# The second norm's sums of three chunks go from VectorE to ScalarE, and the transposes behind them come three groups sooner

## The chip, the cores and the metric

The kernel runs on one core of a Trainium2 chip, as one program. The metric is the time of one execution in microseconds (us), as a median of runs on the chip. A profile of one execution shows every instruction of the engines: TensorE (PE for its products, PEld for its weight loads), VectorE (DVE), ScalarE (ACT), GpSimd (POOL) and the queue of SyncE (SP).

## The reference

A transformer block with adaptive norms, on 2048 rows of 512 numbers, in float32:

```python
mod = (_silu(c) @ w_mod).reshape(c.shape[0], 6, 1, -1)
sa, ca, ga, sb, cb, gb = (mod[:, 0], mod[:, 1], mod[:, 2], mod[:, 3], mod[:, 4], mod[:, 5])
h = _layernorm(x, axis=-1) * (1 + ca) + sa
x = x + ga * _A_ref(h, A_wqkv, A_wo)              # softmax attention, 32 heads of 16
h = _layernorm(x, axis=-1) * (1 + cb) + sb        # the second norm
x = x + gb * _B_ref(h, B_w_gate, B_w_up, B_w_down)  # (silu(h wg) * (h wu)) wd, inner width 1792
return x
```

`_layernorm` subtracts the mean of a row of 512 and divides by the root of its variance plus 1e-5.

## The kernel before, in words

The rows are cut into 4 chunks of 512, each of 4 tiles of 128 rows. After the first norm and the projections (`proj_T`, `proj_v`), the attention runs as one long sequence of steps: 32 units (4 chunks times 8 groups of 4 heads) of 16 steps, and 4 pairs a step. A pair (`pair_of`) issues one score product with its exponential (`score`: TensorE L569, ScalarE L571) and, some 20 steps ahead of it, one product for the row maximum with its reduction (`max_one`: TensorE L521, VectorE L523). The products of the exponentials with v (`pv_step`, L584) follow in bundles of half steps (`pvs`). At the end of a unit `close_unit` copies the result (L588) and queues loads on SP and POOL.

While a chunk's attention runs, the rest of the block for the chunk before it is done between the pairs. That gives two kinds of stretch:

- `plain(steps)`: only attention, in groups of three pairs and then products with v. Four PSUM banks take the products for the maxima in a ring (0 to 3, begun anew by each call of `plain`), three take the scores. A function in `tails` is called in a group between its pairs and its products with v, with the next bank of the ring of four.
- `filled(places, work)`: eight pairs, with products of `work` between them as `places` says, then four half steps of v. Three banks take the maxima here, two the scores, and banks 3 and 6 the outputs of `work`.

For each of the first three chunks the loop at the end of the kernel goes: `plain` up to a fixed step; `out_pair` for tiles 0 and 1 in two filled stretches, then for tiles 2 and 3 in two more (the output projection, L782); `plain(NORM)`, 9 steps or 12 groups; `plain(WIN)`, 3 steps or 4 groups; for the third chunk a further `plain(REST)`; and then the gate, up and down products in filled stretches. The document counts the 16 groups behind the four stretches from 0.

The second norm lies around these. When an `out_pair` is done, `add_o` adds it to x (VectorE L804, two tiles), and `sums` takes mean and variance of a tile (VectorE L808 and L809). `scaled` then loads the first gate weights, forms one over the root in small operations (`norm_scale`: VectorE L740 to L742, then POOL L749 to L754), and normalizes the four tiles on POOL (`normalize`, L761). `turned` transposes a block of 128 columns of the four tiles on TensorE (L766), scales and shifts it on ScalarE (L768), and splits it in a high and a low part on POOL (L769, L770).

Three lists set when such work is issued. `side` gives up one entry behind each pair. `posts` is emptied at the end of each filled stretch (`hook`). `behind` holds entries with a count; at the end of each group and each filled stretch (`turns_behind`, after the products with v) each count falls by one, and an entry whose count reaches zero is issued. Instructions are issued in this written order, and each engine works through its own in that order. The fourth chunk's norm runs alone at the end, with `late` false and VectorE for `norm_scale`.

Of the kernel before, what the change touches and what calls it, by code (L numbers as in the profile page):

```python
# [13 lines left out]
AF = mybir.ActivationFunctionType  # L14
ALU = mybir.AluOpType
# [6 lines left out]
D = 512  # L22
# [4 lines left out]
NK = D // P  # L27
# [6 lines left out]
EPS = 1e-5  # L34
# [5 lines left out]
WIN = 3  # L40
# [7 lines left out]
NORM = 9  # L48
# [53 lines left out]
def block_kernel(ctx, tc, x, wqkv, wo, w_gate, w_up, w_down, c, w_mod, out):  # L102
    nc = tc.nc
# [18 lines left out]
    four, bank, single = Turn(0, 1, 2, 3), Turn(4, 5, 6), Turn(7)  # L122
# [271 lines left out]
    def proj_T(ci, w, m, by=1, aside=False):  # L394
        def job():
            pt = bank("pt")
            col = (0 if w == 0 else D) + m * P

            def post():
                prt = pa0.tile([P, 2, CW], F32R, name="prt", tag="prt", bufs=4)  # L400
                if aside:
                    full = prt[:, 1, :].bitcast(F32)
                    nc.scalar.copy(full, pt)
                    yield
                    nc.gpsimd.tensor_copy(prt[:, 0, :], full)
                    nc.gpsimd.tensor_sub(prt[:, 1, :], full, prt[:, 0, :].bitcast(F32))
                else:
                    nc.scalar.copy(prt[:, 0, :], pt)
                    yield
                    nc.vector.tensor_sub(prt[:, 1, :], pt, prt[:, 0, :].bitcast(F32))  # L410
                yield
                dst = (qd, kd)[w][m * P:(m + 1) * P, :, ci * CW:(ci + 1) * CW]
                nc.sync.dma_start(dst[:, 1 - w:3 - w, :], prt.bitcast(F32))
                nc.sync.dma_start(dst[:, 2 * w, :], prt[:, 0, :].bitcast(F32))
            return mm3(pt, lambda a, k: wqs[a][:, k, col:col + P], lambda b, k: hT[ci][b][:, k, :], NK, by, w == 1), post()
        return job
# [77 lines left out]
    posts, behind = [], []  # L494
# [134 lines left out]
    def tile_mid():  # L629
        return pf.tile([P, 2, CW], F32R, name="mid", tag="mid", bufs=3)  # L630

    def tmp(name):
        return pf.tile([P, CW], F32, name=name, tag="tmp", bufs=4)
# [56 lines left out]
    class Chunk:  # L690
# [45 lines left out]
        def norm_scale(self, eng):  # L736

            mv, rs, a = self.mv, self.rs, self.rs2[:, 0]
            va = mv[:, :, 1]
            nc.vector.tensor_scalar_add(va, va, EPS)  # L740
            nc.vector.tensor_scalar(rs.bitcast(I32), va.bitcast(I32), 1, None, op0=ALU.logical_shift_right)
            nc.vector.tensor_scalar(rs.bitcast(I32), rs.bitcast(I32), -1, 0x5f3759df, op0=ALU.mult, op1=ALU.add)  # L742
            for _ in range(3):
                if eng is nc.vector:
                    eng.scalar_tensor_tensor(a, rs, -0.5, rs, op0=ALU.mult, op1=ALU.mult)
                    eng.tensor_mul(a, a, va)
                    eng.scalar_tensor_tensor(rs, a, 1.5, rs, op0=ALU.add, op1=ALU.mult)
                else:
                    eng.tensor_mul(a, rs, rs)  # L749
                    eng.tensor_mul(a, a, va)  # L750
                    eng.tensor_scalar(a, a, -0.5, 1.5, op0=ALU.mult, op1=ALU.add)
                    eng.tensor_mul(rs, rs, a)
            eng.tensor_mul(self.rs2[:, 1], mv[:, :, 0], rs)
            eng.tensor_scalar_mul(self.rs2[:, 1], self.rs2[:, 1], -1.0)  # L754

        def normalize(self, t, alone=False):
            if alone:
# [39 lines left out]
    def add_o(ch, t0, outs, late):  # L797
        if ch.mv is None:
            ch.mv = pf.tile([P, 4, 2], F32, name="mv2", tag="mv2", bufs=1)
            ch.rs = pf.tile([P, 4], F32, name="rs", tag="rs", bufs=1)  # L800
            ch.rs2 = pf.tile([P, 2, 4], F32, name="rs2", tag="rs2", bufs=1)
        for e in range(2):
            t = t0 + e
            nc.vector.tensor_add(ch.x2[:, t, :], outs[e], ch.x2[:, t, :])  # L804

        def sums(t):
            st = pf.tile([P, 6], F32, name="stt", tag="stt", bufs=2)
            nc.vector.bn_stats(st, ch.x2[:, t, :])  # L808
            nc.vector.bn_aggr(ch.mv[:, t, :], st)  # L809

        for e in range(2):
            if late:
                side.append(lambda t=t0 + e: sums(t))
            else:
                sums(t0 + e)

    def out_pair(ch, t0, outs, halves):
        return accumulate(outs, lambda e, a, k: ch.oT[a][:, k, (t0 + e) * P:(t0 + e + 1) * P],
                          lambda b, k: ch.wo[k // 2][:, b, k % 2, :], NK,
                          lambda: posts.append(lambda: add_o(ch, t0, outs, True)), halves)  # L820
# [53 lines left out]
    side = []  # L874
# [13 lines left out]
    def scaled(ch):  # L888
        ch.load_gu(0)
        ch.norm_scale(nc.gpsimd)  # L890
        ch.nt = [tile_mid().bitcast(F32) for _ in range(2)]
        for t in range(4):
            ch.normalize(t)
# [7 lines left out]
    late = sm.jobs([proj_T(last, *kq[0])] + [(late_t if w == "T" else late_v).pop(0) for w in "TTVTVTTVTTVTTVVVV"])  # L901
# [3 lines left out]
    four, bank = Turn(0, 1, 2, 3, 6, 7), Turn(4, 5)  # L905
# [56 lines left out]
    def pair_of():  # L962
        nonlocal done
        i = done // 4 - 1
        most = 4 * n - 4 * (LEAD - 1)
        h = (ORDER if done < most else (0, 1, 2, 3))[done % 4]
        work = [lambda: score(i + 1, h)]
        if done < most:
            work.insert(1 - h % 2, lambda: max_one(done + 4 * (LEAD - 1)))
        for f in work:  # L970
            f()
        done += 1
        if side:
            side.pop(0)()

    for i in range(-LEAD, -1):
# [7 lines left out]
        if i == -2:  # L984
            four, work = three, bank
# [11 lines left out]
    def pvs(most, by_halves):  # L997

        nonlocal owed
        if by_halves:  # L1000
            most, owed = most + owed, 0
        while most and halves and 4 * halves[0][0] + 8 <= done:
            i, half = halves.pop(0)
            pv_step(i, half)
            most -= 1
            if i % 16 == 15 and half:
                close_unit(i // 16, done // 4 - 1)
                if by_halves:
                    break
        if by_halves and most and halves and 4 * halves[0][0] + 8 <= done:  # L1010
            owed = most

    def turns_behind():
        for b in list(behind):
            b[0] -= 1
            if not b[0]:
                b[1]()
                behind.remove(b)

    def end_steps():  # L1020
        nonlocal ended
        while ended < done // 4:
            after(ended - 1)
            ended += 1

    def plain(steps, tails=()):

        nonlocal four, bank, beside
        beside = False
        assert steps % WIN == 0 and done % 4 == 0  # L1030
        four, bank = Turn(0, 1, 2, 3), Turn(4, 5, 6)
        for w in range(4 * steps // WIN):
            for _ in range(WIN):
                pair_of()
            if w >= 4 * steps // WIN - len(tails):
                tails[w - 4 * steps // WIN](four())
            pvs((HALVES[(w - 2) % 4] if done > 8 else 0) + (w == 4 * steps // WIN - 1), True)
            turns_behind()
            end_steps()
# [30 lines left out]
    for ci in range(last):  # L1070
        plain(STARTS[ci] - done // 4)
        ch = chunks[ci]
        for t0 in (0, 2):
            work = out_pair(ch, t0, outs, True)
            filled(TWO, work)
            filled(TWO, work)
        side.append(lambda: scaled(ch))
        plain(NORM)
        plain(WIN, [lambda tp, k=k: ch.turned(tp, k) for k in range(NK)])
        if ci == last - 1:  # L1080
            plain(REST)
        for _ in range(len(ch.jobs) - (KEEP if ci == last - 1 else 0)):
            job, args = ch.jobs.pop(0)
            if args == (NF // FG - 1, 0):
                plain(WIN)
            work = job(ch, *args, outs, True)
            for places in (TWO, TWO) if job is gate_up else (DOWN,):
                filled(places, work)
# [5 lines left out]
    turns = chain([2, 3, 2, 0, 1, 2, 0], cycle([1, 3, 2, 0]))  # L1094
# [19 lines left out]
    ch, chp = chunks[last], chunks[last - 1]  # L1114
# [10 lines left out]
    for t in range(4):  # L1125
        out_terms(ch, t, banks[t], (NK - 1,))
        if t % 2:
            add_o(ch, t - 1, banks[t - 1:t + 1], False)
# [40 lines left out]
```

## Time and profile before

| | |
|---|---|
| median of 3 runs | 1834.48 us (1833.5 to 1835.62) |
| the profiled execution's own time | 1835.76 us |
| its span in the profile | 1833.9 us |
| mean granted TensorE clock | 0.998 |
| busy: PE, DVE, ACT, POOL | 1821.6, 1530.4, 1241.4, 460.8 us |

A row of a timeline gives the start and the length in us, engine, line, operation, output and input, a count where rows are merged, and in brackets the idle time before it with what ended it. A row of a group of instructions gives the busy time in us, the mean ns of one, and the idle time of the engine before them. The chain is the work that ended last, followed back from the end of the program.

### The profile page before, as it was taken

The numbers are of one execution on the slowest core, as the hardware profiler recorded it, in microseconds if no ns is written. First come the engines' busy times: TensorE is split into PE (matmuls) and PEld (weight loads), VectorE is DVE, ScalarE is ACT, GpSimd is POOL, SyncE is SP. The second block draws the span as 40 slices with busy tenths as digits, with TensorE's granted clock in tenths as the row PEclk, the third lists the DMA queues.
The fourth block names the chain that finished last, engine by engine and source line by source line (L and its number), as shares of the span: only waits on it lengthen the run. The fifth ranks groups of instructions, "written<-read, shape, count | busy, mean of one in ns | idle before, by whom it ended". The sixth has DMA issues, their size and how long they took to land.

```text
span 1833.9 us, 41048 instructions
## 1 busy us (share of the span) xinstructions
PE 1821.6 (99%) x16904; PEld 1199.0 (65%) x16904; DVE 1530.4 (83%) x2578; ACT 1241.4 (68%) x2386; POOL 460.8 (25%) x541
## 2 busy tenths in 40 slices
PE   9999999999999999999999999999999999999999
PEld 7876444444455777776565777776564577767887
DVE  5578999999999888889999888889999988831544
ACT  4223888888877777777878777777878877774211
POOL 3612544565223111111123111111123011130200
PEclk9999999999999999999999999999999999999999
DMA  9784776657845444453544554454643545333642
GB/s 311 281 225 154 180 184 199 168 188 171 220 79 126 102 118 143 118 143 73 146 104 108 133 129 120 119 121 84 163 83 57 112 92 150 139 120 122 272 169 110
DMA packets 80488, 267.63 MB, mean 146 GB/s; under 512 B 19604, under 2 KB 24212, under 8 KB 59620
## 3 DMA queue, kind: packets, MB, share of 16 engines
q1 hardware_dynamic: 61324, 179.71, 34.0%
q0 software_dynamic: 18288, 84.49, 19.3%
q8 instruction: 133, 2.18, 0.5%
q10 hardware_dynamic: 688, 0.80, 0.1%
q14 instruction: 55, 0.45, 0.1%
HBM read 201.85 MB, written 62.13 MB: 144 GB/s over the span
## 4 chain that ended last, share of the span: by engine, by line
PE 82%; DVE 16%; DMA 1%; ACT 0%; issue 0%; SPq 0%; DVEq 0%
PE bank L584 21%; PE bank L782 19%; DVE mx L523 15%; PE bank L569 14%; PE bank L521 11%; PE bank L792 8%; PE bank L211 7%; PE bank L825 1%; PE bank L766 0%; DMA wm_ab<-in_w_mod 0%; DVE stt L808 0%; DMA qop<-mr 0%; PE bank L163 0%; DVE v_flat L856 0%; PE bank L535 0%
## 5 line engine op out<-in xcount | busy, mean ns | idle before, releaser
L523 DVE TENSOR_REDUCE mx<-bank 128x1 f32<-128x512 f32 x2048 | 1274.3, 685 | 108.7 <-PE bank L521 68.0
L569 PE MATMUL bank<-qop,kop 50*128 50x512 f32 x2048 | 728.8, 426 | 2.5 <-DMA qop<-mr 1.6
L521 PE MATMUL bank<-kop,qop 48*128 48x512 f32 x2048 | 727.0, 426 | 2.5 <-DVE mx L523 2.1
L569 PEld LDWEIGHTS bank<-qop,kop 50*128 50x128 f32 x2048 | 343.5, 184 | 169.8 <-issue 53.6
L521 PEld LDWEIGHTS bank<-kop,qop 48*128 48x128 f32 x2048 | 343.9, 185 | 113.3 <-DVE mx L523 68.7
L782 PE MATMUL bank<-act,wgu 64*128 64x512 f32 x1872 | 301.5, 392 | 0.0
L782 PEld LDWEIGHTS bank<-act,wgu 64*128 64x128 f32 x1872 | 196.7, 187 | 24.2 <-issue 0.2
L611 POOL TENSOR_TENSOR on<-o,rb 128x512 f32<-128x512 f32 x31 | 39.8, 1285 | 494.9 <-DMA rb<-d_dr 350.3
L782 PE MATMUL bank<-wd,mid 64*128 64x512 f32 x912 | 133.8, 397 | 0.0
L844 POOL CAST mid<-m 128x512 fp32r<-128x512 f32 x40 | 24.3, 608 | 381.7 <-DVE m L842 239.2
L782 PEld LDWEIGHTS bank<-wd,mid 64*128 64x128 f32 x912 | 87.7, 185 | 16.1 <-ACT first L879 3.1
L211 PE MATMUL bank<-hT,wqs 128*128 128x512 f32 x384 | 94.3, 397 | 0.4 <-DVE wqs L351 0.4
L840 DVE SCALAR_TENSOR_TENSOR q<-th,bank 128x512 f32<-128x512 f32 x56 | 38.3, 683 | 54.1 <-ACT th L836 54.1
L211 PEld LDWEIGHTS bank<-hT,wqs 128*128 128x128 f32 x384 | 70.6, 188 | 18.8 <-issue 3.0
L836 ACT ACTIVATE th<-bank 128x512 f32<-128x512 f32 x56 | 33.2, 594 | 57.9 <-PE bank L792 57.9
L856 DVE TENSOR_TENSOR x<-bank,x 128x512 f32<-128x512 f32 x84 | 53.9, 685 | 18.3 <-PE bank L782 16.7
L842 DVE TENSOR_TENSOR m<-bank,q 128x512 f32<-128x512 f32 x56 | 38.7, 692 | 21.7 <-PE bank L792 19.7
L845 POOL TENSOR_TENSOR mid<-m,mid 128x512 fp32r<-128x512 f32 x40 | 51.5, 1287 | 3.3
L792 PE MATMUL bank<-wd,mid 128*128 128x512 f32 x216 | 51.3, 393 | 0.0
L782 PE MATMUL bank<-wgu,act 64*128 64x512 f32 x288 | 48.0, 394 | 0.1
L211 PE MATMUL bank<-wqs,hT 128*128 128x512 f32 x192 | 48.0, 398 | 0.0
L792 PEld LDWEIGHTS bank<-wd,mid 128*128 128x128 f32 x216 | 40.4, 188 | 8.9
(6298 smaller groups left out, 5139.7 us busy)
## 6 DMA issues: line engine op xcount, KB each, us to landing
wgu<-gu_dr SPq DMA_DIRECT2D x48, 1024.0 KB
wd<-wd_dr SPq DMA_DIRECT2D x28, 1024.0 KB
kop<-kd SPq DMA_DIRECT2D x33, 768.0 KB
kop<-kd POOLq DMA_DIRECT2D x29, 768.0 KB, 8.9
gu_dr<-wgu POOLq DMA_DIRECT2D x14, 1024.0 KB, 13.8
kd<-prt SPq DMA_DIRECT2D x16, 512.0 KB
qd<-prt SPq DMA_DIRECT2D x16, 512.0 KB
kop<-gu_dr SPq DMA_DIRECT2D x8, 1024.0 KB
```

The lines of the kernel that those rows point to most:

```text
L211: nc.tensor.matmul(pt, lhs(a, k), rhs(b, k), start=(n == 0), stop=(n == 3 * nk - 1))
L521: nc.tensor.matmul(pm, qop[u][rows, s, qt * P:(qt + 1) * P], kop[u % 3][rows, s, kc * CW:(kc + 1) * CW], start=True, stop=True)
L523: nc.vector.tensor_reduce(mx[u][:, b, s, qt, kc:kc + 1], pm, op=ALU.max, axis=AX.X)
L569: nc.tensor.matmul(sp, kop[u % 3][rows, h // 2, kt * P:(kt + 1) * P], qop[u][rows, h // 2, :], start=True, stop=True)
L584: nc.tensor.matmul(pv[u][32 * h:32 * h + 32, cols], v_flat[:, e0:e0 + 32], p_[h][:, cols], start=(kt == 0 and half == 0), stop=(kt == 15), ...
L611: mul.tensor_mul(on, o, rb)
L782: nc.tensor.matmul(outs[e], lhs(e, a, k)[rows], rhs(b, k)[rows], start=(ph == 0 and j == 0), stop=(j == z and (ph == 1 or trade is not None)),
L792: nc.tensor.matmul(outs[e], lhs(e, a, k), rhs(b, k), start=(j == 0), stop=(j == z))
L840: nc.vector.scalar_tensor_tensor(q, th, 1.0, outs[0], op0=ALU.add, op1=ALU.mult)
L842: nc.vector.tensor_mul(m32, outs[1], q)
L845: (nc.gpsimd if slow else nc.vector).tensor_sub(mid[:, 1, :], m32, mid[:, 0, :].bitcast(F32))
L856: nc.vector.tensor_add(ch.x2[:, t, :], outs[e], ch.x2[:, t, :])
```

## The change

For the first three chunks the sums of a tile are no longer one VectorE statistic of two instructions but two ScalarE passes over the tile, each of which adds up its outputs into one column: `minus_mean` scales by −1/512 and sums, which gives minus the mean; `squares` takes that as its bias, squares and sums. The passes are put on `behind`, for tiles 0 and 1 with the counts 1, 2, 2, 3 and for tiles 2 and 3 with 1, 2, 3, 4. `scaled` goes from `side` to `behind` with the count 4, that is, behind the fourth group. `norm_scale` divides the sum of squares by 512 in the instruction that adds the 1e-5, and for these chunks leaves out the POOL multiplication by −1. The four calls of `turned` move from the four groups of `plain(WIN)` to the last three of `plain(NORM)` and the first of `plain(WIN)`. The fourth chunk is as before.

```diff
             va = mv[:, :, 1]
-            nc.vector.tensor_scalar_add(va, va, EPS)
+            if eng is nc.vector:
+                nc.vector.tensor_scalar_add(va, va, EPS)
+            else:
+                nc.vector.tensor_scalar(va, va, 1.0 / D, EPS, op0=ALU.mult, op1=ALU.add)
...
             eng.tensor_mul(self.rs2[:, 1], mv[:, :, 0], rs)
-            eng.tensor_scalar_mul(self.rs2[:, 1], self.rs2[:, 1], -1.0)
+            if eng is nc.vector:
+                eng.tensor_scalar_mul(self.rs2[:, 1], self.rs2[:, 1], -1.0)
...
-        for e in range(2):
-            if late:
-                side.append(lambda t=t0 + e: sums(t))
-            else:
+        def minus_mean(t):
+            nc.scalar.activation(tmp("sq"), ch.x2[:, t, :], AF.Identity, scale=-1.0 / D,
+                                 accum_out=ch.mv[:, t, 0:1])
+
+        def squares(t):
+            nc.scalar.activation(tmp("sq"), ch.x2[:, t, :], AF.Square, bias=ch.mv[:, t, 0:1],
+                                 accum_out=ch.mv[:, t, 1:2])
+
+        if late:
+            turns = (1, 2, 2, 3) if t0 == 0 else (1, 2, 3, 4)
+            works = ((minus_mean, t0), (squares, t0), (minus_mean, t0 + 1), (squares, t0 + 1))
+            behind.extend([k, lambda f=f, t=t: f(t)] for k, (f, t) in zip(turns, works))
+        else:
+            for e in range(2):
                 sums(t0 + e)
...
-            if w >= 4 * steps // WIN - len(tails):
-                tails[w - 4 * steps // WIN](four())
+            if w < len(tails) and tails[w]:
+                tails[w](four())
...
-        side.append(lambda: scaled(ch))
-        plain(NORM)
-        plain(WIN, [lambda tp, k=k: ch.turned(tp, k) for k in range(NK)])
+        behind.append([4, lambda: scaled(ch)])
+        tails = [lambda tp, k=k: ch.turned(tp, k) for k in range(NK)]
+        plain(NORM, [None] * NORM + tails[:3])
+        plain(WIN, tails[3:])
```

## The prediction

> **What bounds the kernel now.** I read the page first, for the engines' shares and the chain that ended last.
>
> ```profile
> span 1833.9 us, 41048 instructions
> ...
> PE 1821.6 (99%) x16904; PEld 1199.0 (65%) x16904; DVE 1530.4 (83%) x2578; ACT 1241.4 (68%) x2386; POOL 460.8 (25%) x541
> ...
> PE 82%; DVE 16%; DMA 1%; ACT 0%; issue 0%; SPq 0%; DVEq 0%
> PE bank L584 21%; PE bank L782 19%; DVE mx L523 15%; PE bank L569 14%; PE bank L521 11%; PE bank L792 8%; PE bank L211 7%; PE bank L825 1%; PE bank L766 0%; DMA wm_ab<-in_w_mod 0%; DVE stt L808 0%; DMA qop<-mr 0%; PE bank L163 0%; DVE v_flat L856 0%; PE bank L535 0%
> ```
>
> TensorE carries the chain, VectorE takes 16% of it, and nearly all of that is the row maximum (L523). ScalarE is on it with 0%. So an operation taken from VectorE is worth something only where VectorE ends a wait of TensorE, and an operation given to ScalarE costs something only where ScalarE has no pause. Both must be read in the stage of the change. The second of the three chunks has it at about 940 to 1000 us; the other two run the same order. Its VectorE timeline (start us, us, operation, idle before and releaser):
>
> ```profile
> 942.72 5.23 DVE L523 TENSOR_REDUCE mx<-bank 128x1 f32<-128x512 f32 x8 [1.52 <-PE bank L569]
> 947.87 1.28 DVE L804 TENSOR_TENSOR x<-bank,x 128x512 f32<-128x512 f32 x2
> 949.46 0.69 DVE L523 TENSOR_REDUCE mx<-bank 128x1 f32<-128x512 f32 x1 [0.32 <-PE bank L521]
> 950.07 0.68 DVE L808 BATCH_NORM_STATS2 stt<-x 128x6 f32<-128x512 f32 x1
> 950.78 0.18 DVE L809 BATCH_NORM_AGGREGATE mv<-stt 128x2 f32<-128x6 f32 x1
> 950.88 0.66 DVE L523 TENSOR_REDUCE mx<-bank 128x1 f32<-128x512 f32 x1
> ...
> 957.15 5.23 DVE L523 TENSOR_REDUCE mx<-bank 128x1 f32<-128x512 f32 x8 [1.13 <-PE bank L569]
> 962.30 1.28 DVE L804 TENSOR_TENSOR x<-bank,x 128x512 f32<-128x512 f32 x2
> 963.89 0.69 DVE L523 TENSOR_REDUCE mx<-bank 128x1 f32<-128x512 f32 x1 [0.32 <-PE bank L521]
> 964.50 0.68 DVE L808 BATCH_NORM_STATS2 stt<-x 128x6 f32<-128x512 f32 x1
> 965.22 0.18 DVE L809 BATCH_NORM_AGGREGATE mv<-stt 128x2 f32<-128x6 f32 x1
> 965.32 0.66 DVE L523 TENSOR_REDUCE mx<-bank 128x1 f32<-128x512 f32 x1
> ...
> 967.29 0.16 DVE L740 TENSOR_SCALAR mv<-mv 128x4 f32<-128x4 f32 x1
> ...
> 967.69 0.17 DVE L742 TENSOR_SCALAR rs<-rs 128x4 int32<-128x4 int32 x1
> ...
> 969.69 21.83 DVE L523 TENSOR_REDUCE mx<-bank 128x1 f32<-128x512 f32 x36
> 992.33 1.89 DVE L523 TENSOR_REDUCE mx<-bank 128x1 f32<-128x512 f32 x3 [0.81 <-PE bank L521]
> 994.85 1.89 DVE L523 TENSOR_REDUCE mx<-bank 128x1 f32<-128x512 f32 x3 [0.63 <-PE bank L521]
> 997.33 2.51 DVE L523 TENSOR_REDUCE mx<-bank 128x1 f32<-128x512 f32 x4 [0.60 <-PE bank L521]
> ```
>
> Two regimes are to be seen. A filled stretch of eight pairs is paced by TensorE: its eight maxima need 5.23 us, and VectorE then waits. From 942.72 to 949.46 one took 6.74 us, from 957.15 to 963.89 again 6.74. The one between, from 949.46 to 957.15, took 7.69, and it is the one that holds two of the sums. From 963.89 on come sixteen groups of three pairs without filling work (groups 0 to 15), and there VectorE works back to back until 991.52, at 21.83/36 = 0.61 us a maximum. Only in the last groups, where the transposes lengthen TensorE's part, does it wait again, 0.6 to 0.8 us a group. ScalarE in the same stage:
>
> ```profile
> 961.62 0.59 ACT L571 ACTIVATE pt__11587<-bank 128x512 f32<-128x512 f32 x1
> 963.86 0.60 ACT L571 ACTIVATE pt__11608<-bank 128x512 f32<-128x512 f32 x1 [1.65 <-PE bank L521]
> ...
> 965.31 0.62 ACT L571 ACTIVATE pt__11656<-bank 128x512 f32<-128x512 f32 x1
> ...
> 968.03 0.60 ACT L571 ACTIVATE pt__11683<-bank 128x512 f32<-128x512 f32 x1 [1.13 <-PE bank L569]
> ...
> 970.04 0.22 ACT L540 ACTIVATE nm<-m 128x16 fp32r<-128x16 f32 x1
> ...
> 972.55 0.26 ACT L537 CAST mr<-bank 48x128 fp32r<-48x128 f32 x1
> 972.98 0.60 ACT L571 ACTIVATE pt__11731<-bank 128x512 f32<-128x512 f32 x1 [0.17 <-PE bank L569]
> ...
> 981.39 0.60 ACT L588 COPY o<-bank 128x512 f32<-128x512 f32 x1
> ```
>
> It pauses 1.65 us at the end of a filled stretch, while TensorE multiplies by v; exponentials follow each other at (965.31 − 963.86)/3 = 0.48 us.
>
> **The sums leave the third filled stretch.** Each sum holds VectorE from its start to that of the next maximum: 950.88 − 950.07 = 0.81 us, two of them 1.6. Without them this stretch has the same work as its neighbours, so 7.69 − 6.74 = 0.95 us goes; TensorE is late next. I take 0.94.
>
> **The sums leave groups 0 and 1.** Again 2 × 0.82 = 1.64 us of VectorE (965.32 − 964.50 for one). VectorE is not idle from there to 991.52, so all of it can come off; that is the ceiling. The three small VectorE operations of the scale stay, three groups later.
>
> **ScalarE gets four passes a chunk.** No pass with an accumulator is in this trace. The nearest groups of ScalarE's operations are these (busy us, mean ns):
>
> ```profile
> L768 ACT ACTIVATE h<-bank,modc 128x512 f32<-128x512 f32 x16 | 12.5, 796 | 1.8 <-PE bank L766 1.4 <-POOL kop L770 0.5
> L844 ACT CAST mid<-m 128x512 fp32r<-128x512 f32 x16 | 9.9, 620 | 41.9 <-DVE m L842 41.9
> L879 ACT COPY first<-bank 1x1 f32<-1x1 f32 x76 | 8.2, 147 | 3.9 <-PE bank L782 1.2
> L483 ACT ACT_TABLE_LOAD x1 | 1.3, 1283 | 0.0
> ```
>
> The plain pass of this shape is 0.62, the one with two column operands (scale and bias) 0.80; Square has one, so about 0.71. Handing out the accumulator lies between nothing and a smallest instruction, 0.15. So a pass is 0.6 to 0.95; I take 0.75, from the middle of the first two rows plus a little. It is below no bound: nothing leaves ScalarE, so there is no gain in this term. A tile costs ScalarE 1.5 us where it cost VectorE 0.82.
>
> The Trainium skill (ScalarE: Activation LUTs, "Rules for kernel authors") speaks against such a move: add and multiply belong on VectorE. The trace agrees that the work grows, but it also shows VectorE without a pause here, which that rule does not weigh. By the same page's section "What ACT_TABLE_LOAD costs" the passes are estimated at 613 and 706 ns without the accumulator; three passes are then 0.3 us shorter than mine, and so would the chunk be.
>
> Where they fall: the first mean pass behind the second filled stretch, the first square and second mean behind the third, the second square and third mean behind the fourth. Two passes are 1.5 us against the pause of 1.65, so they are hidden; behind them on ScalarE's queue wait only the next exponentials, and TensorE's next scores wait for those. A mean pass also waits for its addition (L804), which ends about 962.30 + 0.64 = 962.94 for the first tile of the pair; 0.75 more is 963.7, just before the exponential at 963.86. If that cover were gone, each end of a stretch would cost what exceeds 1.65.
>
> The last three passes stand behind groups 0, 1 and 2, and here ScalarE has little room. Twelve exponentials at 0.48, three passes at 0.75, and 0.48 for the two small operations on the maximum's rows (L540, L537), from 963.86 on, end at 963.86 + 5.8 + 2.25 + 0.48 = 972.4; group 4 began at 972.98 before. ScalarE alone thus allows 0.6 us of gain, VectorE 1.64. Three banks of scores let TensorE run ahead of ScalarE, so ScalarE's end doesn't bind outright: I take 1.2, with 0.6 and 1.64 as ends.
>
> **The transposes come three groups sooner.** POOL, and pieces of the chain:
>
> ```profile
> 967.95 0.19 POOL L749 TENSOR_TENSOR rs<-rs 128x4 f32<-128x4 f32 x1 [4.05 <-DVE rs L742]
> ...
> 971.93 3.02 POOL L761 TENSOR_SCALAR mid<-x,rs,rs 128x512 f32<-128x512 f32 x4
> ```
> ```profile
> 982.27 1.00 PE bank L584 x16
> ...
> 994.35 0.43 PE bank L569
> ...
> 995.24 0.59 PE bank L766 x4
> ```
>
> Four transposes (0.59 us) a group are moved, not saved. Are the rows ready? From the end of the small operations (967.69 + 0.17 = 967.86) to the end of the normalizing (971.93 + 3.02 = 974.95) are 7.1 us; one small POOL operation falls away, 6.8. The small operations now follow twelve maxima: 963.89 + 12 × 0.61 + 0.1 for the small maximum of a unit + 0.57 (967.29 to 967.86) = 971.9, rows at 978.7. The new place is ahead of the product with v that stood at 982.27, 1.2 earlier by the term above: 981.1. So 2.4 us of cover. The same call issues the load of the first gate weights on SP. It still stands there ahead of the row transfers of the next maxima, its buffer is free since the fourth stretch, and it is read only behind group 15. POOL's next loads of k and q follow the normalizing as before.
>
> What it costs: before, the last group's transposes took bank 3 and VectorE was waiting, so the next stretch found its banks free. Now the last three groups carry none, and the ring of banks, begun anew, opens with bank 0, which the very last maximum has just used. Three maxima take 1.89 us from the first's start, while TensorE is back after a pair (0.43) and the product with v (1.00): some 0.5 us of waiting. Also group 9 gets a transpose copy (L768) on ScalarE next to the copy of o (981.39). Against it, three groups run at TensorE's pace and not VectorE's, a gain of up to 0.2 each that VectorE gives back later. I take 0.4 of loss, ends 0 and 0.7.
>
> **Sum.** A chunk: −0.94 − 1.2 + 0.4 = −1.74 us; three: −5.2. The profiled execution took 1835.76 us (1.9 more than its span) and comes to 1830.6; it stands 1.3 above the median of the runs, 1834.48, which comes to 1829.3. With all favourable ends −0.95 − 1.64 = −2.6 a chunk, −7.8: 1826.7. With all unfavourable ones −0.94 − 0.6 + 0.7 = −0.84, −2.5: 1832.0.
>
> **Rivals.** *ScalarE becomes the bound.* For it: the 0.6 us above. If a pass is 1.05, the three behind the groups take 0.9 of the 1.2 back, and the two pairs of passes exceed their pause by 0.45 each: −0.94 − 0.3 + 0.9 + 0.4 = +0.06 a chunk, no change, about 1834.7. At 1.25 they take 1.5 back and exceed by 0.85 each: −0.94 + 0.3 + 1.7 + 0.4 = +1.46 a chunk, +4.4: 1838.9, slower. Against it: no row of this shape is over 0.80, and 0.95 was the upper bound.
>
> *Square brings table loads: slower.* A load is 1.283 us (L483). If Square isn't in the table that serves the exponential, each square costs two, 2.57 us, and the exponentials wait behind them: four squares 10.3 us a chunk, of which the pauses hide almost nothing as they are used up already. 10.3 − 1.74 = +8.5 a chunk, +25.7: 1860. It decides from the first load on. Against it: the load of L483 is the last of the trace, ahead of the first exponential, and Exp, Tanh, Identity and Copy alternate behind it without another. By the Trainium skill (ScalarE: Activation LUTs, "Table sets: the hidden batching unit") cheap functions are in every set, though its examples leave Square out; no run yet shows which.
>
> *The rows are late.* Every microsecond beyond the 2.4 of cover stops TensorE at the transposes. At 1.7 us beyond, the gain is eaten: 1834.5. For it: POOL takes 14 small steps in turn. Against it: nothing else stands in its queue.
>
> *VectorE's time isn't worth anything*, because TensorE would be late anyway: then only the third stretch gains, −0.94 + 0.4, −1.6 in all: 1832.9. Against it: the back-to-back 21.83.
>
> **How the numbers follow.** What a measurement of this kernel can tell from no change is about 0.2%, 3.7 us: faster means under 1830.8. The forecast gets 0.66; about 0.57 of that is beyond 3.7 us and 0.09 short of it. ScalarE's bound 0.10, the late rows 0.04, no worth 0.04: all within. Table loads 0.06; a pass of about 1.25 us, or its like in collisions on ScalarE's queue, 0.10. So faster 0.57, same 0.27, slower 0.16. The range runs from the favourable sum to past the cases of no change: 1826.5 to 1836.
>
> **What would show it.** Right: the third filled stretch at 6.7 us, groups 0 to 3 about 1 us shorter, passes of 0.6 to 0.95 us on ScalarE, no L808 row in the chunks but the last, three groups without a VectorE pause after the transposes, and a short wait of L521 for L523 at the next stretch. Wrong: a table load behind L483's; passes over 1 us; TensorE waiting for L761; the stretch still at 7.7.

## The result, and the profile after

The changed kernel took 1830.53 us (median of 9 runs, 1827.91 to 1833.56) against 1834.48 before (9 runs, 1833.12 to 1837.04). The ratio is 0.9977 with a 95% interval of 0.9969 to 0.9986, that is 2.6 to 5.7 us less. 1829.3 was forecast, 5.2 us less. The profiled execution took 1832.23 us, with a span of 1830.4.

The page after:

```profile
span 1830.4 us, 41073 instructions
...
PE 1819.1 (99%) x16904; PEld 1196.7 (65%) x16904; DVE 1523.4 (83%) x2554; ACT 1256.3 (69%) x2434; POOL 459.7 (25%) x538
...
PE 88%; DVE 8%; DMA 2%; ACT 1%; issue 0%; SPq 0%; DVEq 0%; ACTq 0%
```

VectorE lost 7 us of busy time and 24 instructions, ScalarE gained 15 us and 48 instructions: 24 passes and as many reads of the accumulator, which the profile lists by themselves. The groups of ScalarE's instructions that are new (busy us, mean ns of one):

```profile
L820 ACT ACTIVATE sq<-x,mv 128x512 f32<-128x512 f32 x12 | 8.9, 742 | 0.0
L816 ACT ACTIVATE sq<-x 128x512 f32<-128x512 f32 x12 | 7.7, 638 | 2.7 <-DVE x L808 2.4
L820 ACT ACTIVATION_READ_ACCUMULATOR sq<-x,mv 128x1 f32 x12 | 2.6, 220 | 0.0
L816 ACT ACTIVATION_READ_ACCUMULATOR sq<-x 128x1 f32 x12 | 2.4, 202 | 0.0
```

The second chunk's stage on VectorE, to be held against the timeline of the prediction:

```profile
942.00 5.25 DVE L523 TENSOR_REDUCE mx<-bank 128x1 f32<-128x512 f32 x8 [1.53 <-PE bank L521]
947.16 1.28 DVE L808 TENSOR_TENSOR x<-bank,x 128x512 f32<-128x512 f32 x2
948.76 2.52 DVE L523 TENSOR_REDUCE mx<-bank 128x1 f32<-128x512 f32 x4 [0.32 <-PE bank L521]
...
955.50 5.24 DVE L523 TENSOR_REDUCE mx<-bank 128x1 f32<-128x512 f32 x8 [1.51 <-PE bank L521]
960.66 1.28 DVE L808 TENSOR_TENSOR x<-bank,x 128x512 f32<-128x512 f32 x2
962.26 3.68 DVE L523 TENSOR_REDUCE mx<-bank 128x1 f32<-128x512 f32 x6 [0.32 <-PE bank L569]
965.86 0.21 DVE L528 TENSOR_REDUCE m<-mx 128x16 f32<-128x64 f32 x1
965.98 1.88 DVE L523 TENSOR_REDUCE mx<-bank 128x1 f32<-128x512 f32 x3
968.01 1.89 DVE L523 TENSOR_REDUCE mx<-bank 128x1 f32<-128x512 f32 x3 [0.15 <-PE bank L521]
...
970.49 10.96 DVE L523 TENSOR_REDUCE mx<-bank 128x1 f32<-128x512 f32 x18
981.90 1.89 DVE L523 TENSOR_REDUCE mx<-bank 128x1 f32<-128x512 f32 x3 [0.45 <-PE bank L569]
984.41 1.89 DVE L523 TENSOR_REDUCE mx<-bank 128x1 f32<-128x512 f32 x3 [0.62 <-PE bank L521]
986.90 3.68 DVE L523 TENSOR_REDUCE mx<-bank 128x1 f32<-128x512 f32 x6 [0.60 <-PE bank L569]
990.80 6.37 DVE L523 TENSOR_REDUCE mx<-bank 128x1 f32<-128x512 f32 x10 [0.22 <-PE bank L521]
```

The third stretch, 948.76 to 955.50, is as long as its neighbours, 6.74 us. In the groups the sums are gone, VectorE now waits a little for TensorE (0.15 at 968.01), and the pauses of the groups with transposes have moved to 981.90 to 986.90, with almost none behind. ScalarE in group 0 and at the start of group 1:

```profile
963.20 0.60 ACT L571 ACTIVATE pt__11627<-bank 128x512 f32<-128x512 f32 x1
963.68 0.73 ACT L820 ACTIVATE sq<-x,mv 128x512 f32<-128x512 f32 x1
964.29 0.21 ACT L820 ACTIVATION_READ_ACCUMULATOR sq<-x,mv 128x1 f32 x1
964.38 0.60 ACT L571 ACTIVATE pt__11634<-bank 128x512 f32<-128x512 f32 x1
```

Exponentials otherwise start 0.48 us apart. The square pass between two of them puts the next one off by 964.38 − 963.68 = 0.70 us. The chain of the profile, followed back from 985 us, runs from 962.24 to 969.34 through ScalarE alone:

```profile
962.24 0.59 ACT pt__11615 L571
...
963.80 0.70 ACT sq L820 x2
...
965.96 0.61 ACT sq L816 x2
...
968.14 0.53 ACT sq L820
968.67 0.67 ACT pt__11687 L571
```

From the first exponential of group 0 to that of group 4 ScalarE is busy for 8.16 of 8.23 us. So here it sets the pace, and no longer VectorE; even so these four groups are 0.89 us shorter than before, where they took 9.12.

To compare kernels I take three lengths in each chunk, each from the start of one exponential (L571) to the start of a later one: the third filled stretch (8 pairs), the sixteen groups (48 pairs), and the 8 pairs behind these. Chunks one, two, three; us. The rows below the second are the kernels of the experiments:

| | third stretch | sixteen groups | next 8 pairs |
|---|---|---|---|
| before | 7.69, 7.70, 7.70 | 33.66, 33.43, 33.42 | 6.73, 6.75, 4.59 |
| the change | 6.74, 6.75, 6.74 | 32.39, 32.37, 32.35 | 7.10, 6.76, 4.91 |
| sums only | 6.74, 6.74, 6.74 | 32.42, 32.39, 32.37 | 6.74, 6.75, 4.58 |
| transposes only | 7.68, 7.71, 7.70 | 33.40, 33.40, 33.39 | 7.10, 6.74, 4.91 |
| passes twice | 7.87, 7.88, 7.86 | 34.90, 37.81, 34.77 | 7.10, 6.74, 4.90 |
| passes spread | 6.74, 6.75, 6.73 | 32.19, 32.20, 32.19 | 6.73, 6.75, 4.59 |
| other opening bank | 6.74, 6.75, 6.73 | 32.36, 32.37, 32.35 | 6.73, 6.74, 4.59 |
| no sums of tiles 2, 3 | 6.74, 6.76, 6.74 | 31.84, 31.84, 31.82 | 6.77, 6.74, 4.59 |
| tiles 0, 1 on VectorE | 7.70, 7.69, 7.69 | 32.41, 32.39, 32.37 | 6.75, 6.72, 4.59 |
| behind the longer v | 6.74, 6.74, 6.73 | 32.27, 32.25, 32.24 | 6.73, 6.74, 4.59 |

These lengths repeat within 0.05 us from kernel to kernel, while whole executions scatter by some 5 us. Part of that scatter lies ahead of the first chunk: the first unit's copy (L588), before anything that differs, stands 2.0 us earlier to 2.1 us later than before's in these profiles. A part of this is TensorE's granted clock. From the first exponential to that copy before took 49.5 us, the change 49.6 and sums only 50.8, and in these three the clock stood at 0.5 for 3.4, 3.4 and 6.8 us between 212 and 219 us; the other seven kept 1.00 there and took 46.6 to 47.8. By the table the change gives −1.85, −2.00 and −1.71 us, together −5.6. The copies of units (L588), which also see what VectorE still has in hand behind the third chunk, give −5.3. In both, 0.25 us of the first chunk is a slower clock in before (shown under "Transposes only"), and not the change's. Both lie in the interval of the runs.

### The profile page after: what moved, and what is told of

Its sections match the earlier page's. It is cut to its first block, busy times and chain, and to the rows that moved or that the text cites. A ratio compares the mean times of both kernels' runs of the same rounds, so it can differ in the third digit from the quotient of the medians.

```text
span 1830.4 us, 41073 instructions
## 1 busy us (share of the span) xinstructions
PE 1819.1 (99%) x16904; PEld 1196.7 (65%) x16904; DVE 1523.4 (83%) x2554; ACT 1256.3 (69%) x2434; POOL 459.7 (25%) x538
## 4 chain that ended last, share of the span: by engine, by line
PE 88%; DVE 8%; DMA 2%; ACT 1%; issue 0%; SPq 0%; DVEq 0%; ACTq 0%
PE bank L584 24%; PE bank L786 20%; PE bank L569 16%; PE bank L521 13%; DVE mx L523 8%; PE bank L211 7%; PE bank L796 7%; DMA wm_ab<-in_w_mod 0%; PE bank L770 0%; DMA qop<-mr 0%; DMA kop<-o_dr 0%; PE bank L163 0%; DMA rb<-d_dr 0%; ACT sq L820 0%; PE bank L839 0%
```

## The experiments

**Sums only.** The change with the transposes back in the last four groups.

```diff
-        plain(NORM, [None] * NORM + tails[:3])
-        plain(WIN, tails[3:])
+        plain(NORM)
+        plain(WIN, tails)
```

> The sums and the scale as in the change, the transposes back in the last four groups. My theory: the whole gain comes from the sums, and the move of the transposes gives a part back, through the ring of banks. Third filled stretch 6.74 us instead of 7.69, the sixteen groups 1.5 us shorter than before in each of the three chunks (33.4 to 31.9), no wait at the start of the next stretch: -7.3 us against before, about 1.5 to 2 better than the change. Rival: the earlier transposes carry a part of the gain; then this kernel is slower than the change, -3 or less against before.

1828.4 us against 1834.74, ratio 0.9962 (0.9948 to 0.9975), −4.6 to −9.5 us. The groups are as short as in the change (expected 31.9, measured 32.4), and the stretch behind them is not lengthened. So the sums carry the whole gain, together with the later place of the scale, which no run moves by itself. VectorE in the second chunk:

```profile
971.26 18.36 DVE L523 TENSOR_REDUCE mx<-bank 128x1 f32<-128x512 f32 x30
990.43 1.88 DVE L523 TENSOR_REDUCE mx<-bank 128x1 f32<-128x512 f32 x3 [0.81 <-PE bank L569]
992.94 1.89 DVE L523 TENSOR_REDUCE mx<-bank 128x1 f32<-128x512 f32 x3 [0.63 <-PE bank L521]
995.43 2.51 DVE L523 TENSOR_REDUCE mx<-bank 128x1 f32<-128x512 f32 x4 [0.60 <-PE bank L521]
```

The same three pauses as before stand at the end again, and VectorE enters the next stretch waiting.

**Transposes only.** Before, with the change's two lines of `tails` and the rule for them in `plain`; the sums and `scaled` stay on `side`.

> The sums on VectorE as before, the scale in group 0 as before, and only the transposes three groups sooner. My theory: nothing gained, +0.1 us in each of the first two chunks, +0.65 in the third, whose next groups open with the bank that the last maximum has just used: +0.9 against before, no difference that the runs can tell; third stretch at 7.7. Rival: the move brings a gain of its own, -1.5 or more against before.

1835.69 against 1834.74, ratio 1.0003 (0.9994 to 1.0012). By the copies of units the three chunks gave +0.12, +0.07 and +0.50 us, near the +0.1, +0.1 and +0.65 expected. The first chunk's groups are 0.26 shorter than before, but not by the transposes. Before's first chunk ran part of them at a lower granted clock. In these rows of 2 us the columns are the stretch, its length, the busy time (and number) of PE, PEld, DVE, ACT and POOL, then the granted clock as a share of full speed, the share of DMA and GB/s:

```profile
560.00:562.00 2.00, 1.96 (x16) 0.90 (x18) 1.97 (x6) 1.60 (x4) 0.00 (x0) 0.84 0.00 0
562.00:564.00 2.00, 2.00 (x18) 1.15 (x10) 1.93 (x7) 0.27 (x1) 0.99 (x5) 0.50 0.04 8
564.00:566.00 2.00, 2.00 (x24) 0.87 (x23) 2.00 (x5) 1.41 (x4) 1.39 (x7) 0.81 0.00 0
```

Here it stayed at 1.00, and the groups took the 33.40 of the other chunks.

**Passes twice.**

```diff
-            behind.extend([k, lambda f=f, t=t: f(t)] for k, (f, t) in zip(turns, works))
+            behind.extend([k, lambda f=f, t=t: (f(t), f(t))] for k, (f, t) in zip(turns, works))
```

> The change with each of ScalarE's passes issued twice; the second writes the same again. My theory: ScalarE has hardly room left. Behind the second stretch about +0.3 us, behind the third and fourth 2.6 us of passes against a pause of 1.65, so +1.0 each, and in groups 0 to 2 another 1.9 us of passes, of which nearly all shows: 2 us more in the sixteen groups than the change. Together about +4.3 a chunk against the change, +13 in all, some +8 against before. Rival: ScalarE at 69% has room; then within 2 us of the change.

1847.47 against 1834.74, ratio 1.0067 (1.0054 to 1.0079). ScalarE has no room: the third stretch is 1.13 us longer than in the change, the groups 2.4 to 2.5 in chunks one and three, against 1.0 and 2 expected. The second chunk's groups took 5.4 more, and that part was not expected. The stretches of three us there:

```profile
975.00:978.00 3.00, 1.94 (x19) 0.84 (x17) 2.00 (x6) 2.97 (x9) 0.52 (x3) 1.00 0.00 0
978.00:981.00 3.00, 3.00 (x18) 1.33 (x18) 1.98 (x3) 1.88 (x5) 2.07 (x12) 0.53 0.02 5
981.00:984.00 3.00, 3.00 (x24) 1.08 (x22) 1.89 (x3) 1.57 (x3) 3.00 (x4) 0.50 0.00 0
984.00:987.00 3.00, 3.00 (x28) 1.44 (x26) 2.15 (x4) 1.87 (x4) 1.21 (x3) 0.83 0.18 30
```

TensorE had been busy for 1.94 of 3 us, waiting for exponentials, and then ran some 7 us at about half the clock, now itself the slowest: ScalarE is busy for 1.6 to 1.9 of 3 us there. In the first and the third chunk a drop fell where ScalarE still set the pace (busy for 2.97 of each 3 us): 6.8 us at 0.50 from 561.9 in the first, 3.4 us from 1381 in the third. Their groups took 34.90 and 34.77, so twice the time at half the clock made next to no difference there. Against these the second chunk's drop cost about 3 us.

**Passes spread.** Sums only, with the three passes further apart.

```diff
-            turns = (1, 2, 2, 3) if t0 == 0 else (1, 2, 3, 4)
+            turns = (1, 2, 2, 3) if t0 == 0 else (1, 3, 5, 7)
...
-        behind.append([4, lambda: scaled(ch)])
+        behind.append([7, lambda: scaled(ch)])
```

> The transposes back in the last four groups, and the three passes of tiles 2 and 3 behind groups 1, 3 and 5 instead of 0, 1 and 2, the scale behind group 6. My theory: spread like this the passes hide entirely, the sixteen groups lose the full 1.64 us of VectorE: -2.6 a chunk, -7.8 against before, 0.5 better than with the passes in groups 0 to 2; the rows are ready 2 us or more before the transposes. Rival: ScalarE's passes were hidden already, no difference from the kernel with the sums alone.

1829.34 against 1834.74, ratio 0.9967 (0.9955 to 0.998). The groups came to 32.19, 0.2 shorter than with the passes in groups 0 to 2, and not to the 31.8 that hiding them entirely would give.

**Other opening bank.** The change, with the rings begun at the bank that was used longest ago.

```diff
-            plain(REST)
+            plain(REST, ids=(1, 2, 3, 0))
+        three = Turn(1, 2, 0)
```

`plain` takes the order of its ring as `ids` for this; those two lines are left out here.

> The change, with the rings of banks started at the bank that was used longest ago: the third chunk's further groups open with bank 1, the filled stretches behind each chunk's groups likewise. My theory: what the early transposes cost is the opening bank. In the third chunk VectorE's pause of 0.58 us at the start of the further groups goes (-0.5 us there), in the first chunk the stretch behind the groups is back from 7.1 to 6.75 (-0.35), the second chunk has no such wait and keeps its time: the three chunks' stages come to the -6.2 us that the sums alone gave, about 0.9 less than the change's. Rival: the cost lies in group 9, where the transposes meet the copy of o; then nothing changes against the change.

1830.05 against 1833.85, ratio 0.9969 (0.9957 to 0.998). The next 8 pairs are back at 6.73 and 4.59, the copies of units around the three stages give −2.21, −1.94 and −2.29 us, −6.4 together instead of −5.3. (From the first unit's copy to the last it is −6.0 instead of −5.1; what is lost between the stages wasn't followed up.) VectorE at the end of the third chunk's groups, first in the change, then here:

```profile
1393.98 3.82 DVE L523 TENSOR_REDUCE mx<-bank 128x1 f32<-128x512 f32 x6 [0.22 <-PE bank L569]
1398.38 3.68 DVE L523 TENSOR_REDUCE mx<-bank 128x1 f32<-128x512 f32 x6 [0.58 <-PE bank L569]
```
```profile
1393.71 7.51 DVE L523 TENSOR_REDUCE mx<-bank 128x1 f32<-128x512 f32 x12 [0.23 <-PE bank L569]
```

The pause of 0.58 us is gone, and the groups keep their length (32.36, 32.37 and 32.35): the loss of the earlier transposes was the opening bank, and not the copy of o in group 9.

**No sums of tiles 2 and 3.** Sums only, with a POOL write of a constant in place of the four passes of these tiles.

> The kernel with the sums alone (transposes in the last four groups), but the sums of tiles 2 and 3 are left out altogether; a constant stands in their place. It shows what the sixteen groups take with neither VectorE nor ScalarE doing sums. My theory: 1.3 to 1.64 us a chunk less than before in the groups, against 1.05 with the passes behind groups 0 to 2 and 1.24 with them spread: ScalarE's passes there cost 0.3 to 0.6 us a chunk; about -7.4 against before. Rival: the passes are free and VectorE's sums never were worth 1.64; then the groups stay at 1.05.

1826.76 against 1833.85, ratio 0.9953 (0.9934 to 0.9972). The groups take 31.84, 1.59 less than the 33.43 of before: that is what VectorE's two sums held, 1.64 by the prediction. Against sums only, whose transposes stand in the same groups, the passes on ScalarE cost 32.39 − 31.84 = 0.55 of it, 0.35 when spread.

**Tiles 0 and 1 on VectorE.** Sums only, but these two tiles are summed as before on `side`.

> The kernel with the sums alone, but tiles 0 and 1 are summed on VectorE as before (their mean and variance are not brought to the form that the scale expects). My theory: the third stretch is at 7.7 us again, the groups as with the sums alone, so -1.05 to -1.25 us a chunk, -3.4 against before, and the other 0.95 a chunk is the third stretch's. Rival: with more room behind the stretches the groups gain more, or the third stretch stays at 6.74.

1832.31 against 1833.85, ratio 0.9986 (0.9977 to 0.9996). The third stretch is at 7.69 again and the groups keep 32.4: the two halves of the gain are separate, 0.95 and 1.05 us a chunk.

**Behind the longer products with v.** As the spread passes, with `turns` (1, 4, 7, 8) and a count of 8 for `scaled`.

> As the kernel with the passes spread, but behind groups 2, 5 and 6, in which two half steps of v follow each other (1.0 us of TensorE in which no score is made), and the scale behind group 7. My theory: ScalarE's passes cost what of them exceeds the pause left by the product with v; with the longer products the groups come from 32.2 us to 31.9, close to the 31.84 without these passes: -2.5 a chunk, -7.6 against before; the rows are ready some 1 us before the transposes. Rival: the 0.35 us that were left are no matter of the pause but of reading the same tiles, or of more instructions; then the groups stay at 32.2.

1827.43 against 1834.94, ratio 0.9964 (0.9952 to 0.9977), beside sums only the best of the versions that compute the whole; the runs can't tell these two and the spread one apart. The groups stayed at 32.25, so my theory of the pause fell: it is not the length of the product with v that decides what a pass costs. What the remaining 0.35 to 0.4 us a chunk consist of is open. In the second chunk the first eight groups took 14.74 us with the passes spread, ScalarE busy for 14.37 of it and VectorE for 14.54; without the passes of tiles 2 and 3 they took 14.48, ScalarE busy for 12.60 and VectorE for 14.38. With the passes neither engine has room left, which would fit a loss, but no run here separates the passes' time on ScalarE from the reading of the same tiles.

## Why the prediction was right

The forecast was 1829.3 with a range of 1826.5 to 1836; measured 1830.53, faster by 0.23%. Step by step:

- **The third stretch**, −0.94 a chunk: −0.95 in all three, and the experiment with tiles 0 and 1 on VectorE ties it to tiles 0 and 1. TensorE was late next, as said.
- **The sums in the groups**, ceiling 1.64: 1.59. **What ScalarE takes back**, 0.44, to a net 1.2: 0.55, to a net of 1.04 (1.06 in the change). The pass was put at 0.75 us; it takes 0.64 or 0.74 by itself and puts the next instruction off by 0.70 for the square and 0.61 for the mean (954.41 to 954.93, and 0.09 for its read). So the price of a pass was a little high. The step that failed here is "ScalarE's end doesn't bind outright": in groups 0 to 2 the chain lies on ScalarE. The prediction's own sum for ScalarE holds with the measured prices, 12 × 0.48 + 0.70 + 0.61 + 0.71 + 0.48 = 8.26 us against the 8.23 from group 0 to group 4. So ScalarE allowed 0.89 us there and not 0.6, and only some 0.15 more came in the later groups. That 1.2 came near is partly luck: a pass put too dear and a bound taken too lightly offset each other. By the Trainium skill (ScalarE: Activation LUTs, "What ACT_TABLE_LOAD costs") the two were estimated at 613 and 706 ns; the rows show 638 and 742, the accumulator's read not counted. The three passes of the groups, two squares and a mean, come to 2.03 us by that estimate, 0.2 less than the prediction's 2.25 and not 0.3.
- **The pauses behind the filled stretches** hide two passes: yes. ScalarE's four instructions between the exponentials of the third and fourth stretch:

```profile
953.71 0.72 ACT L820 ACTIVATE sq<-x,mv 128x512 f32<-128x512 f32 x1
954.32 0.20 ACT L820 ACTIVATION_READ_ACCUMULATOR sq<-x,mv 128x1 f32 x1
954.41 0.62 ACT L816 ACTIVATE sq<-x 128x512 f32<-128x512 f32 x1
954.93 0.20 ACT L816 ACTIVATION_READ_ACCUMULATOR sq<-x 128x1 f32 x1
955.47 0.60 ACT L571 ACTIVATE pt__11526<-bank 128x512 f32<-128x512 f32 x1 [0.34 <-PE bank L521]
```

  0.34 us of the pause are left. Doubled, they don't fit, and the third stretch grows by 1.13.
- **The transposes**, +0.4 a chunk: the mechanism was right, the size was not the same for all. It costs 0.35 us in the first chunk, nothing in the second, and by the copies of units some 0.5 to 0.8 in the third (−1.48 in the change, −2.1 with sums only, −2.29 with the other bank). I had each next stretch open with bank 0, the one just used. That holds for the third chunk's further groups; the filled stretches share one ring of three that goes on through the whole kernel, and by a count of its uses in the code opened with bank 2 in the first chunk and bank 1 in the second. Bank 1 is the one used longest ago, which fits the second chunk's zero. That the three come to some 0.3 on average, near the 0.4, is luck.
- **The rows**: expected 14.8 us behind the first maximum of group 0 (978.7 − 963.89), they were ready at 974.15 + 3.03 = 977.18, 14.9 behind 962.26. TensorE began the transposes 2.6 us later, at 979.80, and its short wait was for another:

```profile
974.15 3.03 POOL L765 TENSOR_SCALAR mid<-x,rs,rs 128x512 f32<-128x512 f32 x4
```
```profile
979.80 0.63 PE L770 MATMUL bank<-ident,mid 128*128 128x128 f32 x4 [0.20 <-DVE mx L523]
```

- **The rivals**: no table load stands behind the one of L483 (at 109.1 us in the change's trace). That cheap functions are in every set, as the Trainium skill has it (ScalarE: Activation LUTs, "Table sets: the hidden batching unit"), fits Square too for the set that is in use here; other sets were not tried. ScalarE did become the bound, in groups 0 to 2, but with passes of 0.61 to 0.71 us, well below the 1.05 at which the gain would have gone; the doubled passes show what more of them costs. The rows were not late.

The sum of the terms was −5.2, the stages show −5.3 to −5.6 (0.25 of it before's clock) and the runs −2.6 to −5.7. That adding and multiplying belong on VectorE (the Trainium skill, ScalarE: Activation LUTs, "Rules for kernel authors") was right on the work (ScalarE's 1.3 us a tile for 0.82) and gave the wrong direction, since VectorE was the one without a pause.

## What to carry to other kernels

Ask of a moved operation not what it costs but which engine is without a pause at that place, and put it into the other's real pauses: two passes behind a product of 1.9 us were free, three between dense groups gave back a third of what they had freed. When work is moved within a ring of buffers, count through which buffer the next loop opens with; the order in which two rings are begun decided about 1 us here. Parts that a whole run can't separate (0.3 us in 1830) can be told apart by lengths between two recurring instructions of the trace, which here repeat within 0.05 us.

## What the runs showed of the hardware that was not expected

An accumulator is handed out by an instruction of its own, listed with 0.20 to 0.22 us, of which only 0.09 puts off the next pass (964.29 to 964.38). TensorE's granted clock fell to 0.5 now and then, each time for 3.4 or 6.8 us, the end of the run aside: once in before's first chunk, at a cost of about 0.25 us, and in every chunk with doubled passes, at about 3 us where TensorE was the slowest engine by then and at next to nothing where ScalarE was. Between 212 and 219 us it did so in three of the ten profiles. No run here shows what brings it about. With doubled passes TensorE was busy for only 2.56, 1.94 and 1.89 of the 3 us ahead of the three drops, but before's drop followed 5 us (556 to 561) with 4.96 busy, and in the doubled kernel the stretch from 966 to 969, again 1.89 of 3, was followed by the full clock.
